# Two row tiles taken in by columns, and a second weight group moved forward

## The chip, the cores and the metric

The kernel runs on one core of one Trainium2 chip. The metric is the device time of one execution in microseconds (us). The core has five engines, each with its own instruction queue that it works through in order: TensorE (PE in the profile), VectorE (DVE), ScalarE (ACT), GpSimd (POOL) and SyncE (SP), which here only issues DMA transfers. Engines wait for each other by semaphores; a transfer runs beside them once it is issued.

## The reference, cut to what matters

```python
# x: 2048 x 512; all in float32
xn = layernorm(x)                                  # per row, no weights
q, k, v = split(xn @ wqkv)                         # wqkv: 512 x 1536, 32 heads of 16
s = attention(q, k, v) @ wo                        # each position sees 8 positions, 2 apart
z = gelu(xn @ w_in)                                # 512 x 1792, two halves z1, z2
g = w_sp @ layernorm(z2) + b_sp                    # w_sp: 2048 x 2048
out = x + s * silu((z1 * g) @ w_out)
```

Only the first two lines matter for this change: the row normalisation of `x` and its product with `wqkv`.

## The kernel before

**Tiles and products.** The 2048 rows are taken as 16 row tiles (`NT`) of 128 rows and 512 columns. A product of float32 precision is made from three matmuls of a rounded "high" part and a "low" remainder: high by high, high by low, low by high. ScalarE makes each high part (a copy with rounding), VectorE each low part (source minus high). A product of one row tile with one weight group (`wqkv` has three groups of 512 columns, `NG`) is 4 blocks of the contraction by 3 = 12 matmuls of 128x512, into one PSUM bank. In the product of a tile, the matmuls that read the tile's high part come first; the first one that reads its low part is the third (in `product`, lines 393 to 397).

**Two ways in.** TensorE wants `xn` with the contraction (the columns of `x`) on the partitions.

- Row tiles 0 to `OPEN - 1` (0 to 5 before) are loaded by rows (`load_x`, line 209). VectorE takes mean and variance (`stats_x`), centres the rows (tiles 0 to 3) or centres and scales them (tiles 4 and 5) in `normal_x`; TensorE transposes them in four pieces (`turned_x`, line 234), ScalarE copies the high part out of PSUM (line 235), VectorE makes the low part (`low_x`, line 240). For tiles 0 to 3 (`JC = 4`) the scale is applied when the product is evicted.
- The later tiles come in twice: by rows for their statistics alone (`fetch_rows`, line 257, and `row_stats`, lines 261 and 262), and by columns from a transposed copy of `x` in DRAM (`fetch_cols`, line 268, tiles `xT`). The statistics of a group of three or four tiles then go round by DRAM: `rows_ready` (lines 272 and 273) turns variances into scales, with the power on GpSimd; `rows_out` transposes them on VectorE (line 244) and stores them with four DMAs (line 246, `mv_d`); `rows_in` (line 277) loads them back, spread over all partitions, as `mr`. With `xT` and `mr` there, `column_tile` does two VectorE operations (line 286) and the high copy on ScalarE (line 289), and `low_x` the low part on VectorE (line 240).

**Order.** Instructions issued under `pin(...)` keep the order in which the code is written, on every engine that they are on. So the place of a statement in this part of the code is its place in the queue of VectorE, ScalarE and SP. The matmuls, evictions and stores inside `pair(g, j0)` (the products of tiles `j0` and `j0 + 1` with weight group `g`) are not pinned; a scheduler places them between the pinned ones when the kernel is built. Buffers: six row tiles for statistics (tag `xs`), four column tiles (tag `xT`), two `mr`. A column tile can be loaded when the tile four before has had its low part taken. Each DMA of SP and ACT also uses one of eight semaphores in turn and waits for the transfer eight before it.

After `opening` (line 301), which takes the first tiles in and starts their products, the code alternates `pair`, statistics and column tiles up to tile 15. Then come the rest of the products with the three groups, the z branch, the spatial product with `w_sp`, and the two output projections; attention runs on VectorE and GpSimd beside them.


## Time and profile before

| | before |
|---|---|
| time, median of 3 runs | 694.22 us (693.69 to 698.0) |
| the profiled execution: its own time, its span | 692.16 us, 690.3 us |
| TensorE busy, of the span | 684.8 us, 99%, 3080 matmuls |
| VectorE / ScalarE / GpSimd busy | 619.8 (90%) / 276.0 (40%) / 216.8 us (31%) |
| DMA | 182.43 MB, mean 264 GB/s |

The span runs from the first instruction to the last of the profiled execution; the rest of its own time, 1.86 us, lies around it. Times in the trace count from the start of the span. A row of the timeline reads: start, duration, engine, line, operation, tile written <- tiles read, and in brackets how long the engine was idle before and what ended it. Matmuls are pipelined, so their durations overlap; the distance between two starts is what one costs. The engine "SPq" or "POOLq" in a row is that engine's issue of a DMA.

### The profile page before, as it was taken

To read this page: it belongs to the slowest core of one execution; us is meant where nothing else is said; L and a number is where in the kernel's file an instruction comes from. 1 tells how busy PE (TensorE), PEld (TensorE's weight loads), DVE (VectorE), ACT (ScalarE), POOL (GpSimd) and SP (SyncE) were. 2 spreads that over 40 slices of the span, in tenths; PEclk is the share of its full clock that TensorE was granted. 3 is DMA by queue.
4 is the path that set the end of the run, shared out by engine and by line. 5 is a ranking of instruction groups with operands and counts; after the bars stand their busy time and mean duration, and the time that the engine had idled before them with its cause. 6 is when DMAs were issued, how large, how long until landed. Compare 5 with 4: busy or idle time off the path is not lost.

```text
span 690.3 us, 9237 instructions
## 1 busy us (share of the span) xinstructions
PE 684.8 (99%) x3080; PEld 572.5 (83%) x3080; DVE 619.8 (90%) x866; ACT 276.0 (40%) x458; POOL 216.8 (31%) x242
## 2 busy tenths in 40 slices
PE   9999999999999999999999999999999999999997
PEld 7888888888888899888888888888888888888886
DVE  6677869999989979798999999999999999999765
ACT  4343334224424256785434544432444444211432
POOL 3105837373443221223323222224021202552320
PEclk9999999999999999999999999999999999999999
DMA  8759899969999865267797859677576692663996
GB/s 281 257 180 299 292 359 388 334 218 370 404 414 355 324 207 180 97 207 249 232 397 285 328 195 319 202 237 262 171 270 238 219 325 89 205 186 126 308 309 252
DMA packets 102223, 182.43 MB, mean 264 GB/s; under 512 B 9184, under 2 KB 45152, under 8 KB 102176
## 3 DMA queue, kind: packets, MB, share of 16 engines
q1 hardware_dynamic: 56624, 102.21, 43.7%
q0 software_dynamic: 13824, 52.24, 20.9%
q10 hardware_dynamic: 31728, 27.40, 11.9%
q8 instruction: 24, 0.39, 0.2%
q14 instruction: 23, 0.19, 0.1%
HBM read 122.49 MB, written 59.32 MB: 263 GB/s over the span
## 4 chain that ended last, share of the span: by engine, by line
PE 99%; DMA 0%; DVE 0%; issue 0%
PE g L848 39%; PE qkv L395 6%; PE qkv L396 6%; PE qkv L397 6%; PE z L751 4%; PE z L750 4%; PE z L715 4%; PE z L714 4%; PE b L1089 4%; PE b L1091 4%; PE b L1090 4%; PE z L716 4%; PE z L749 3%; PE s L1089 2%; PE s L1091 2%; PE s L1090 2%
## 5 line engine op out<-in xcount | busy, mean ns | idle before, releaser
L643 POOL TENSOR_TENSOR pv<-pv 128x1024 f32<-128x1024 f32 x29 | 69.6, 2399 | 94.3 <-DVE pv L630 83.0
L583 DVE TENSOR_TENSOR pr<-k,q 128x2048 f32<-128x2048 f32 x32 | 74.7, 2333 | 1.5 <-DMA k<-qkv_d 1.4
L630 DVE TENSOR_TENSOR pv<-v,lg 128x2048 f32<-128x2048 f32 x32 | 74.5, 2329 | 0.6
L590 DVE TENSOR_REDUCE lg<-pr 128x128 f32<-128x2048 f32 x32 | 72.9, 2279 | 0.1
L657 POOL DMA_DIRECT2D o_d<-tt x32 | 17.9, 560 | 148.0 <-DVE tt L656 104.5
L443 ACT ACTIVATE stage<-qkv 128x512 f32<-128x512 f32 x40 | 23.0, 590 | 31.9 <-DMA qkv_d<-stage 20.2
L1100 ACT ACTIVATE bt<-b 128x512 f32<-128x512 f32 x16 | 9.5, 596 | 45.7 <-PE b L1091 45.7
L830 POOL DMA_DIRECT2D ol<-o_d x32 | 17.7, 554 | 28.9 <-DVE o_1l L204 6.0
L720 ACT ACTIVATE z1t<-z 128x512 f32<-128x512 f32 x28 | 15.5, 596 | 25.8 <-DMA z_d<-z1t 14.1
L761 DVE BATCH_NORM_STATS2 zst<-zt 128x6 f32<-128x448 f32 x32 | 19.3, 610 | 7.0 <-ACT zt L752 7.0
L751 PE MATMUL z<-w_0h,BIG 128*128 128x512 f32 x64 | 25.0, 391 | 0.0
L750 PE MATMUL z<-w_0l,BIG 128*128 128x512 f32 x64 | 25.0, 391 | 0.0
L286 DVE TENSOR_TENSOR xT<-xT,mr 128x512 f32<-128x512 f32 x20 | 14.9, 743 | 11.2 <-DMA mr<-mv_d 6.9
L775 ACT ACTIVATE zt<-zt,nmz,mvz 128x896 f32<-128x896 f32 x16 | 17.4, 1128 | 18.0 <-POOL nmz L769 18.0
L767 POOL TENSOR_TENSOR mvz<-mvz,nhalf 128x2 f32<-128x2 f32 x8 | 9.3, 1157 | 47.3 <-DVE mvz L764 47.3
L749 PE MATMUL z<-w_0h,BIG 128*128 128x512 f32 x60 | 23.3, 389 | 0.0
L648 DVE TENSOR_TENSOR pv<-pv 128x512 f32<-128x512 f32 x32 | 22.9, 714 | 0.0
L752 ACT ACTIVATE zt<-z 128x512 f32<-128x512 f32 (+1 forms) x32 | 16.0, 537 | 15.8 <-DMA sums_d<-sa 12.2
L751 PE MATMUL z<-w_1h,BIG 128*128 128x384 f32 x64 | 21.5, 336 | 0.0
L750 PE MATMUL z<-w_1l,BIG 128*128 128x384 f32 x64 | 21.5, 335 | 0.0
L403 POOL TENSOR_TENSOR sb<-sa,sb 128x512 f32<-128x512 f32 x12 | 19.8, 1647 | 5.4 <-DMA sb<-in_w_sp 5.0
L202 ACT ACTIVATE BIG<-zl 128x512 fp32r<-128x512 f32 x20 | 12.4, 630 | 20.7 <-DVE zl L921 20.6
(480 smaller groups left out, 2262.6 us busy)
## 6 DMA issues: line engine op xcount, KB each, us to landing
qkv_d<-stage ACTq DMA_DIRECT2D x24, 512.0 KB
v<-qkv_d POOLq DMA_DIRECT2D x14, 704.0 KB, 5.0
k<-qkv_d POOLq DMA_DIRECT2D x13, 704.0 KB, 6.3
sums_d<-sa POOLq DMA_DIRECT2D x14, 512.0 KB, 7.6
sums_d<-sb POOLq DMA_DIRECT2D x14, 512.0 KB, 9.4
z_d<-z1t ACTq DMA_DIRECT2D x14, 512.0 KB
zl<-z_d SPq DMA_DIRECT2D x12, 512.0 KB
tr<-t_d SPq DMA_DIRECT2D x12, 384.0 KB
```

The lines of the kernel that those rows point to most:

```text
L395: nc.tensor.matmul(pq, xh[:, k], wh, start=k == 0, stop=False)
L396: nc.tensor.matmul(pq, xh[:, k], wl, start=False, stop=False)
L397: nc.tensor.matmul(pq, xl[:, k], wh, start=False, stop=k == KB - 1)
L583: line(nc.vector.tensor_tensor(pr, taps(ks[u], j0), qb.unsqueeze(1).to_broadcast([P, W, NJ * CS]), op=ALU.mult))
L590: line(nc.vector.tensor_reduce(lgs[u][:, j0 * HS : (j0 + NJ) * HS].rearrange("p i w -> p w i"), pr.rearrange("p w (i d) -> p w i d", d=DH) ...
L630: line(nc.vector.tensor_tensor(pv.rearrange("p w (i d) -> p w i d", d=DH), taps(vs[u], j0).rearrange("p w (i d) -> p w i d", d=DH), lgs[u] ...
L643: eng.tensor_tensor(pv[:, 0:4], pv[:, 0:4], pv[:, 4:8], op=ALU.add)
L749: nc.tensor.matmul(pz, xh[:, k], wh, start=k == 0, stop=False)
L750: nc.tensor.matmul(pz, xh[:, k], wl, start=False, stop=False)
L751: nc.tensor.matmul(pz, xl[:, k], wh, start=False, stop=k == KB - 1)
L848: nc.tensor.matmul(pg, z[a], w[b], start=start and i == 0, stop=stop and i == 2, skip_group_check=seeded)
L1089: nc.tensor.matmul(pp[:, cols], hi, wh, start=k == 0, stop=False)
```

## The change

`OPEN` goes from 6 to 4: row tiles 4 and 5 no longer come in by rows and through TensorE. They are the first group of the second way in: fetched by rows for statistics, fetched by columns, their statistics sent round by DRAM on their own (`rows_out((4, 6))`, `rows_in(4, 6)`), then `column_tile(4)` and `column_tile(5)`. So that TensorE has products meanwhile, `pair(1, 0)` and `pair(1, 2)` (tiles 0 to 3 with the second weight group) are written ahead of `pair(0, 4)`. All later groups (6 to 8, 9 to 12, 13 to 15) keep their members and their order on VectorE, but their loads get new places among the others in SP's queue.

```diff
-OPEN = 6
+OPEN = 4
...
         times(1, (3, 0, 1))
-        x += [load_x(j) for j in range(3, OPEN)]
-        for j in range(OPEN, OPEN + 4):
+        x.append(load_x(3))
+        for j in (4, 5):
             fetch_rows(j)
         raw1 = [fetch(wqkv[:, 1, k, :], GC, f"wqkv_1_{k}") for k in range(3)]
...
-        for j in range(3, OPEN):
-            xt = x[j]
-            stats_x(j, xt)
-            low_x(j - 1, p)
-            normal_x(j, xt)
-            if j - 1 < JC:
-                rstd_x(j - 1)
-            first.append(mm(f"qkv_0_{j - 1}"))
-            left.append(12)
-            times(j - 1, *[(k, 0, i) for i in range(2) for k in range(KB)])
-            p = turned_x(j, xt)
-            times(j - 1, *[(k, 1, 0) for k in range(KB)])
-            row_stats(OPEN + j - 3)
-        low_x(OPEN - 1, p)
-        for j in range(10, 13):
+        for j in (4, 5):
+            fetch_cols(j)
+        for j in (6, 7):
             fetch_rows(j)
-        for j in range(6, 10):
-            fetch_cols(j)
-        rows_ready(6, 9)
-        rows_out((6, 9))
+        stats_x(3, x[3])
+        low_x(2, p)
+        normal_x(3, x[3])
+        rstd_x(2)
...
+        for j in (4, 5):
+            row_stats(j)
+        rows_ready(4, 6)
+        low_x(3, p)
+        times(3, *[(k, 1, 0) for k in range(KB)])
+        rstd_x(3)
+        rows_out((4, 6))
...
     pair(0, 0)
-    rows_in(6, 9)
-    for j in range(13, NT):
-        fetch_rows(j)
+    fetch_rows(8)
+    rows_in(4, 6)
+    fetch_rows(9)
+    for j in (6, 7):
+        fetch_cols(j)
     pair(0, 2)
+    for j in range(6, 9):
+        row_stats(j)
+    rows_ready(6, 9)
+    column_tile(4)
+    rows_out((6, 9))
+    column_tile(5)
+    low_x(4, cols[4])
+    for j in range(10, 13):
+        fetch_rows(j)
+    rows_in(6, 9)
+    fetch_cols(8)
+    pair(1, 0)
     for j in range(9, 13):
         row_stats(j)
     rows_ready(9, 13)
-    pair(0, 4)
+    low_x(5, cols[5])
     column_tile(6)
     rows_out((9, 13))
+    pair(1, 2)
     column_tile(7)
     low_x(6, cols[6])
-    for j in range(10, 12):
-        fetch_cols(j)
+    fetch_cols(9)
     rows_in(9, 13)
-    pair(1, 0)
+    for j in range(13, NT):
+        fetch_rows(j)
+    pair(0, 4)
     for j in range(13, NT):
         row_stats(j)
     rows_ready(13, NT)
     column_tile(8)
     low_x(7, cols[7])
-    fetch_cols(12)
+    for j in (10, 11):
+        fetch_cols(j)
     rows_out((13, NT), (0, JC))
-    pair(1, 2)
+    pair(1, 4)
     column_tile(9)
     low_x(8, cols[8])
     rows_in(13, NT)
+    fetch_cols(12)
     column_tile(10)
     low_x(9, cols[9])
-    pair(1, 4)
```

What that does to the queues, in the rows of the built programs (the numbers in a name are group and tile; a last number is only the buffer's).

TensorE, right after the eight matmuls that read the high part of tile 3, before the change (`xt_4` is the transpose of tile 4, `qkv_0_3` the product of tile 3 with the first weight group):

```order
L316 MATMUL qkv_0_3_267<-wqkv_0_3l_168,BIG_98 128x512
L234 MATMUL xt_4_276<-ident_85,x_4_209 128x128 x4
L316 MATMUL qkv_0_3_267<-wqkv_0_0h_130,BIG_98 128x512
L316 MATMUL qkv_0_3_267<-wqkv_0_1h_144,BIG_98 128x512
L316 MATMUL qkv_0_3_267<-wqkv_0_2h_150,BIG_98 128x512
L316 MATMUL qkv_0_3_267<-wqkv_0_3h_167,BIG_98 128x512
L316 MATMUL qkv_0_4_296<-wqkv_0_0h_130,BIG_98 128x512
```

and the same place with the change (`L397` to `L399` are the lines 395 to 397 of before):

```order
L316 MATMUL qkv_0_3_255<-wqkv_0_3l_168,BIG_98 128x512
L397 MATMUL qkv_1_0_354<-wqkv_1_0h_285,BIG_98 128x512
L397 MATMUL qkv_1_1_368<-wqkv_1_0h_285,BIG_98 128x512
L397 MATMUL qkv_1_2_408<-wqkv_1_0h_285,BIG_98 128x512
L397 MATMUL qkv_1_3_422<-wqkv_1_0h_285,BIG_98 128x512
L316 MATMUL qkv_0_3_255<-wqkv_0_0h_130,BIG_98 128x512
```

The transposes are gone, and tiles 0 to 3 begin with the second weight group where tile 4 stood; tile 4 follows 48 matmuls of that group later.

SP's queue, from the stores of the statistics of tiles 6 to 8 (`mvt_6`) to the load of those of tiles 9 to 12 (`mr_9`), before the change:

```order
L246 DMA mv_d_83<-mvt_6_335 6x32 x4
L277 DMA mr_6_361<-mv_d_83 128x768
L257 DMA x_13_363<-in_x 128x512
L257 DMA x_14_365<-in_x 128x512
L257 DMA x_15_367<-in_x 128x512
L246 DMA mv_d_83<-mvt_9_407 8x32 x4
L268 DMA xT_10_417<-in_x_t 128x512
L268 DMA xT_11_419<-in_x_t 128x512
L277 DMA mr_9_421<-mv_d_83 128x1024
```

and with it:

```order
L246 DMA mv_d_83<-mvt_6_333 6x32 x4
L257 DMA x_10_343<-in_x 128x512
L257 DMA x_11_345<-in_x 128x512
L257 DMA x_12_347<-in_x 128x512
L277 DMA mr_6_349<-mv_d_83 128x768
L268 DMA xT_8_351<-in_x_t 128x512
L246 DMA mv_d_83<-mvt_9_401 8x32 x4
L268 DMA xT_9_441<-in_x_t 128x512
L277 DMA mr_9_443<-mv_d_83 128x1024
L257 DMA x_13_445<-in_x 128x512
L257 DMA x_14_447<-in_x 128x512
L257 DMA x_15_449<-in_x 128x512
```

The rows of tiles 13 to 15 stood ahead of the stores of `mvt_9`, and now stand behind the load of `mr_9`.

VectorE with the change, behind the column operations of tile 6, from the transpose of the statistics of tiles 9 to 12 on; before, the same instructions stand in the same order:

```order
L244 STREAM_TRANSPOSE mvt_9_401<-mvx_94 128x32
L286 TENSOR_TENSOR xT_7_313<-xT_7_313,mr_6_349 128x512 x2
L240 TENSOR_TENSOR BIG_98<-xT_6_311,BIG_98 128x4x128
L261 BN_STATS st_13_481<-x_13_445 128x6
L262 BN_AGGR mvx_94<-st_13_481 128x2
L261 BN_STATS st_14_484<-x_14_447 128x6
L262 BN_AGGR mvx_94<-st_14_484 128x2
L261 BN_STATS st_15_487<-x_15_449 128x6
L262 BN_AGGR mvx_94<-st_15_487 128x2
L272 TENSOR_SCALAR mvx_94<-mvx_94 128x3
L286 TENSOR_TENSOR xT_8_351<-xT_8_351,mr_6_349 128x512 x2
L240 TENSOR_TENSOR BIG_98<-xT_7_313,BIG_98 128x4x128
```

The low part of tile 7 (the last row) stands behind the statistics of tiles 13 to 15, and these now read transfers that are issued behind `mr_9`.

More of the change, by code (lines that the diff above doesn't have):

```diff
@@ L367, in opening @@
         pin(nc.sync.dma_start(raw1[3], wqkv[:, 1, 3, :]))
[L368 to L387 removed]
+        for j in (4, 5):
+            fetch_cols(j)
+        for j in (6, 7):
+            fetch_rows(j)
+        stats_x(3, x[3])
+        low_x(2, p)
+        normal_x(3, x[3])
+        rstd_x(2)
+        left.extend([12, 12])
+        first.append(mm("qkv_0_2"))
+        times(2, *[(k, 0, i) for i in range(2) for k in range(KB)])
+        p = turned_x(3, x[3])
+        times(2, *[(k, 1, 0) for k in range(KB)])
+        first.append(mm("qkv_0_3"))
+        times(3, *[(k, 0, i) for i in range(2) for k in range(KB)])
+        for j in (4, 5):
[5 more added lines that the diff above has]
+        rows_out((4, 6))
         return raw1
@@ L441, in pair @@
         for j in (j0, j0 + 1):
-            pq = first[j] if g == 0 and j < OPEN - 1 else product(g, j, wgs[g])
+            pq = first[j] if g == 0 and j < OPEN else product(g, j, wgs[g])
             nc.scalar.activation(
@@ L457 @@
     pair(0, 0)
+    fetch_rows(8)
[3 more added lines that the diff above has]
+        fetch_cols(j)
+    pair(0, 2)
+    for j in range(6, 9):
[7 more added lines that the diff above has]
+        fetch_rows(j)
     rows_in(6, 9)
-    for j in range(13, NT):
-        fetch_rows(j)
-    pair(0, 2)
+    fetch_cols(8)
+    pair(1, 0)
     for j in range(9, 13):
@@ L517 @@
     for g in range(1, NG):
-        for j in range(OPEN if g == 1 else 0, NT, 2):
+        for j in range(OPEN + 2 if g == 1 else 0, NT, 2):
             if g == 1 and j == NT // 2:
```

## The prediction

> **What bounds the kernel now.** I read the page's busy times and chain first, then TensorE's waits, then the windows of the first 60 us, then each engine's timeline there.
>
> ```profile
> PE 684.8 (99%) x3080; PEld 572.5 (83%) x3080; DVE 619.8 (90%) x866; ACT 276.0 (40%) x458; POOL 216.8 (31%) x242
> PE 99%; DMA 0%; DVE 0%; issue 0%
> PE warm L296 <- POOL ident masks.py:199: 1.3, 1, 1.3
> PE xt L234 <- DVE x L228: 0.3, 1, 0.3
> 16.95:45.00 28.05, 28.05 (x128) 22.85 (x128) 19.17 (x45) 11.27 (x19) 4.19 (x5) 1.00 0.74 241
> 45.00:60.00 15.00, 15.00 (x68) 12.43 (x67) 9.84 (x16) 5.34 (x10) 2.35 (x3) 1.00 0.76 220
> ```
>
> The chain that ended last is TensorE alone. The next two rows are all its waits: 1.6 us, both before the first product. A busy share of 99% could hide gaps, since matmuls overlap, so the pace must be read from starts:
>
> ```profile
> 30.82 0.39 PE L396 MATMUL qkv<-wqkv_1l,BIG 128*128 128x512 f32 x1
> ...
> 40.11 0.39 PE L396 MATMUL qkv<-wqkv_0l,BIG 128*128 128x512 f32 x1
> ```
>
> Between these two rows lie 41 steps: 9.29 / 41 = 0.2266 us per matmul, without a hole. So the kernel is one TensorE stream. A matmul taken out pays its step in full, and a pause put in costs its length in full, wherever it falls. The change can do only these two things. The windows (TensorE, weight loads, VectorE, ScalarE, GpSimd, clock, DMA share, GB/s) say that VectorE is busy 19.17 of 28.05 us where the change acts, and the DMA engines 74%.
>
> **What it removes from TensorE.** Eight transposes, four for each of tiles 4 and 5.
>
> ```profile
> 16.95 0.41 PE L316 MATMUL qkv<-wqkv_0h,BIG 128*128 128x512 f32 x1
> ...
> 18.81 0.60 PE L234 MATMUL xt<-ident,x 128*128 128x128 f32 x4
> 19.17 0.48 PE L316 MATMUL qkv<-wqkv_0h,BIG 128*128 128x512 f32 x1
> 19.48 0.40 PE L316 MATMUL qkv<-wqkv_1h,BIG 128*128 128x512 f32 x1
> L234 PE MATMUL xt<-ident,x x24: 270/273/476, 5.4 to 22.4; 128*128 128x128 f32 x24
> ```
>
> Four transposes take 19.17 - 18.81 = 0.36 us, and the matmul behind them a step of 0.31 instead of 0.23: 0.44 us a tile, 0.89 us for two. The number of 512-wide matmuls stays, so **-0.9 us** is all there is to gain.
>
> The last row gives 273 ns as the length of one transpose. The Trainium skill (TensorE: Matmul & The Clock Gate, Part 4: PE-mode transpose) states some 275 ns for one in a kernel's context, and the row agrees; eight of those would be an estimated 2.2 us. The starts decide here, since the four overlap.
>
> **What it adds elsewhere.** VectorE loses two normalisations (0.54 each) and gains four column operations (about 0.7 each) and one transpose of 0.2: +1.9 us, beside 8.9 idle us in the first window; nothing if no order is disturbed, 1.9 at most. ScalarE keeps its two high copies. GpSimd exchanges two powers for one. SP gains two column loads and a read-back of 256 KB each and four small stores, 0.8 MB against 182; their bytes are nothing, their places in the queue are not.
>
> **What it moves: the low part of tile 7.** In VectorE's queue the statistics of tiles 13 to 15 stand ahead of the column operations of tile 8 and of the low part of tile 7, before and after. Before, their rows were long there. Now SP issues them behind the read-back of tiles 9 to 12, which waits for stores that follow tile 6's column operation, which needs the read-back of tiles 6 to 8, and that follows the one of tiles 4 and 5. Three trips by DRAM in a row, one of them new. TensorE waits for the low part at its 15th matmul from tile 6 on. Both sides of that meeting can be dated.
>
> *When TensorE needs it.* Up to 16.95, the first matmul of tile 3, the streams are alike. From there on stand 12 for tile 3, 48 for tiles 0 to 3 with the second group, 48 for tiles 4 and 5 with both, 12 for tile 6 and 2 for tile 7: 122 x 0.2266 = 27.6 us, so at **44.6 us**.
>
> *When VectorE has it.* The rows:
>
> ```profile
> 16.84 0.69 DVE L240 TENSOR_TENSOR BIG<-xt,BIG 128x512 fp32r<-128x512 f32 x1 [1.17 <-ACT BIG L235]
> 17.45 0.54 DVE L197 TENSOR_SCALAR x<-x,mvx 128x512 f32<-128x512 f32 x1
> 19.70 0.15 DVE L220 TENSOR_SCALAR mvx<-mvx 128x1 f32<-128x1 f32 x1
> 19.93 0.55 POOL L221 TENSOR_TENSOR mvx<-mvx,nhalf 128x1 f32<-128x1 f32 x1 [1.26 <-DVE mvx L220]
> 25.08 0.21 DVE L244 STREAM_TRANSPOSE mvt<-mvx 128x32 f32<-128x32 f32 x1 [0.98 <-POOL mvx L273]
> 25.32 1.34 SPq L246 DMA_DIRECT2D mv_d<-mvt  x4
> 28.57 0.35 SPq L277 DMA_DIRECT2D mr<-mv_d  x1
> 28.97 1.82 SPq L257 DMA_DIRECT2D x<-in_x  x3
> 33.47 1.42 DVE L286 TENSOR_TENSOR xT<-xT,mr 128x512 f32<-128x512 f32 x2 [2.39 <-DMA mr<-mv_d]
> 34.81 0.20 DVE L244 STREAM_TRANSPOSE mvt<-mvx 128x32 f32<-128x32 f32 x1
> ```
>
> 1. The statistics of tiles 4 and 5 leave VectorE (L244) behind the low part of tile 3 (17.45 where L197 stood) and one more power: 19.93 - 19.70 + 0.55 = 0.78, and 0.04 to the transpose: 18.3.
> 2. One trip. From the transpose to the issue of the read-back 28.57 - 25.08 = 3.49; from there to the first column operation 4.90, and 4.09 in the second trip (41.99 to 46.08, below). So 7.6 to 8.4; I take 7.6, since this read-back is the smallest. Tile 4: 25.9.
> 3. Column operation to the next transpose 34.81 - 33.47 = 1.34, and a second trip: tile 6 at 25.9 + 1.3 + 7.6 = 34.8. (The statistics of tiles 9 to 12 stand ahead of it in VectorE's queue; their rows are issued in the same trip, and could add up to 1 us.)
> 4. Again 1.34, and 3.49 to the issue of the third read-back: 39.6.
> 5. The rows of tile 15, the third load behind it:
>
> ```profile
> 41.99 0.33 SPq L277 DMA_DIRECT2D mr<-mv_d  x1
> 46.08 1.42 DVE L286 TENSOR_TENSOR xT<-xT,mr 128x512 f32<-128x512 f32 x2 [4.51 <-DMA mr<-mv_d]
> 51.67 0.75 SPq L277 DMA_DIRECT2D mr<-mv_d  x1
> 57.79 1.42 DVE L286 TENSOR_TENSOR xT<-xT,mr 128x512 f32<-128x512 f32 x2 [3.91 <-DMA xT<-in_x_t]
> 0.72 0.38 SPq L209 DMA_DIRECT2D x<-in_x  x1
> 3.92 0.69 DVE L214 BATCH_NORM_STATS2 st<-x 128x6 f32<-128x512 f32 x1 [2.91 <-DMA x<-in_x]
> ```
>
>    The first load behind a read-back was waited for until 57.79 - 51.67 = 6.1 us after the latter's issue; two more at 1.82 / 3 = 0.61 make 7.3. A load with nothing ahead takes 3.92 - 0.72 = 3.2, and it is issued 0.4 + 1.2 later: 4.8. I take the middle, 6.1: the same traffic, but nothing stands in front of the read-back. 45.7.
> 6. From there:
>
> ```profile
> 38.44 0.66 DVE L261 BATCH_NORM_STATS2 st<-x 128x6 f32<-128x512 f32 x1
> 39.13 0.18 DVE L262 BATCH_NORM_AGGREGATE mvx<-st 128x2 f32<-128x6 f32 x1
> 39.35 0.17 DVE L272 TENSOR_SCALAR mvx<-mvx 128x3 f32<-128x3 f32 x1
> 39.43 1.41 DVE L286 TENSOR_TENSOR xT<-xT,mr 128x512 f32<-128x512 f32 x2
> 40.76 0.68 DVE L240 TENSOR_TENSOR BIG<-xT,BIG 128x512 fp32r<-128x512 f32 x1
> ```
>
>    These are the statistics of tile 15, the columns of tile 8 and the low part of tile 7 of before: 40.76 + 0.68 - 38.44 = 3.0 us. So **48.7 us**.
>
> TensorE would pause 48.7 - 44.6 = **4.1 us** there. Before, tile 6 began at
>
> ```profile
> 42.60 0.39 PE L395 MATMUL qkv<-wqkv_0h,BIG 128*128 128x512 f32 x1
> ```
>
> so the low part of tile 7 was needed at 42.60 + 14 x 0.2266 = 45.8 and was there at 41.4. That cover of 4.4 us is what the change spends.
>
> **Other places.** Tile 4's high part, at 25.9 + 1.4 + 0.6 = 27.9, meets a need at 16.95 + 60 x 0.2266 = 30.5; its low part (29.4) one at 31.4. Tile 5's low part, behind the statistics of tiles 9 to 12, comes at 35 to 36 against 36.8: close, but a wait there would shorten the later one by as much. The second group's weights are loaded earlier and split from 16.8 on, and TensorE's first use is at 18.8. After the pause VectorE needs 1.34 + 0.60 = 1.9 us a tile and TensorE 12 x 0.2266 = 2.7, so it gains ground; the column loads of tiles 11 to 13 are issued behind the same low part and come about when they are needed: 0 to 1 us more, of which I count nothing. The rest of the program has the same work in nearly the same order.
>
> **The sum.** -0.9 + 4.1 = +3.2. The profiled execution took 692.16 us (span 690.3, and 1.86 around it): 695.4 on its scale. The median of the runs, 694.22, is 2.06 higher than that execution, so on its scale **697.4 us**, +0.5%. Bounds of the pause: with both trips at 8.4 and 7.3 in step 5, 51.6 and so 7.0 us; with stores that land at once and loads of 3.2 (a trip of 0.24 + 1.34 + 3.2 = 4.8) the low part is there at about 40, and there is no pause.
>
> **Rivals.**
>
> *No pause.* The early traffic is thinner than before (rows of tiles 8 to 15 no longer stand in front of everything), so the trips may be short enough. Each of the three must then save 1.4 us on the shortest row. For it: the read-backs are small. Against it: the undelayed trip of the trace took 8.4, 7.6 is already pieced from its parts and the next one's, and the windows show the DMA engines 74% busy. It gives -0.9: 693.3.
>
> *A long pause, and a slow TensorE behind it.* After its idle start TensorE runs slower for a while:
>
> ```profile
> 5.40 1.12 PE L234 MATMUL xt<-ident,x 128*128 128x128 f32 x4 [0.28 <-DVE x L228]
> 6.31 1.06 PE L296 MATMUL warm<-ident 128*128 128x128 f32 x4
> ```
>
> Four transposes took 6.31 - 5.40 = 0.91 us there against 0.36 later; TensorE had begun at 1.35. For it: 8.4 is a trip as measured, and two such make the upper bound. If that pause brings the same 5.0 us back at 0.36 / 0.91 of the pace, 3.0 us are lost on top: -0.9 + 7.0 + 3.0 = +9.1, or 703.3. It decides from a pause long enough to count as idle; the trace shows no pause in the stream that could tell how long that is, and the granted clock reads 1.00 in all windows, so no row tells when the pace falls. The Trainium skill (TensorE: Matmul & The Clock Gate, Part 1: The HAM clock gate) puts it at one idle window of about 3.4 us that runs free of the kernel, and the slow pace at half for about as long; an estimate by that is 1.7 us lost, seldom at a pause of 4.1. The slow start agrees with it; no run here shows the rest.
>
> *It doesn't matter, because the order after it moves too.* The scheduler puts some later instructions elsewhere, at the end too, where TensorE's last late step hung on a copy of ScalarE:
>
> ```profile
> 677.80 0.61 ACT L202 ACTIVATE o_3h<-ol 128x512 fp32r<-128x512 f32 x1
> 678.47 0.50 PE L1089 MATMUL s<-BIG,o_3h 128*128 128x512 f32 x1
> 678.81 0.39 PE L1090 MATMUL s<-BIG,o_3h 128*128 128x512 f32 x1
> ```
>
> A step of 0.34 instead of 0.23: the order was just in time there. I give such places 0.3 us either way in all: 697.1 to 697.7.
>
> **Chances.** The pause of 2 to 6 us, as forecast: 0.62, 1 to 5 us slower. No pause, or one under 2 us: 0.24. The long one: 0.14, of which rather more than half passes 1%. A measurement of this kernel can tell about 1% (6.9 us) from no change, so faster by more than that 0.01 (the gain is bounded at 0.9), within 0.90, slower 0.09. The range: downward to the case without a pause, 693.3, and half the 2 us between the two scales, so 692.5; upward to the pause at its upper bound, 700.3, and a little of the lost pace: 701.
>
> **What would show it.** In the changed kernel's profile: 16 transposes of line 234; among TensorE's waits one of about 4 us near 44.6 for the low part of a column tile (line 240), at the second product behind tile 5's; on VectorE an idle stretch of 4 us or more before statistics (line 261), ended by the rows of `x`; the read-back's issue near 39.6. If TensorE's waits stay as they are, steps 2 to 5 are too long; if the pause is at tiles 4 or 5, the first trip is. A longer step between matmuls behind the pause would be the second rival.

## The result, and the profile after

The change made the kernel slower: 711.18 us (median of 6 runs, 709.93 to 713.73) against 693.96 us for the kernel before, a ratio of 1.0239 (95% interval 1.020 to 1.0277). The profiled execution took 711.61 us, its span grew from 690.3 to 709.6. Forecast were 697.4 us and a range of 692.5 to 701.

The page's busy times and the chain that ended last; then all of TensorE's waits (total us, how many, the longest):

```profile
PE 688.5 (97%) x3072; PEld 574.0 (81%) x3072; DVE 619.0 (87%) x868; ACT 278.3 (39%) x458; POOL 216.8 (31%) x241
PE 58%; DVE 17%; DMA 16%; issue 4%; ACT 3%; POOL 1%; SPq 1%; ACTq 0%; DVEq 0%
```

```profile
PE qkv L399 <- DVE BIG L240: 7.9, 2, 7.4
PE g L867 <- ACT g L885: 6.3, 2, 4.9
PE warm L296 <- POOL ident masks.py:199: 1.3, 1, 1.3
PE z L768 <- ACT z1t L739: 0.8, 1, 0.8
PE xt L234 <- DVE x L228: 0.7, 1, 0.7
PE qkv L316 <- ACT BIG L235: 0.2, 1, 0.2
```

TensorE, alone on the chain before, holds 58% of it now. The first wait is the forecast one, for the low part of a column tile (line 240). The second and the fourth stand hundreds of microseconds behind the change; for all such places the forecast had 0.3 us either way.

The pause in TensorE's timeline, and what follows it:

```profile
45.18 0.39 PE L398 MATMUL qkv<-wqkv_0l,BIG 128*128 128x512 f32 x1
52.97 0.79 PE L399 MATMUL qkv<-wqkv_0h,BIG 128*128 128x512 f32 x1 [7.40 <-DVE BIG L240]
53.56 0.63 PE L397 MATMUL qkv<-wqkv_1h,BIG 128*128 128x512 f32 x1
53.99 0.63 PE L398 MATMUL qkv<-wqkv_1l,BIG 128*128 128x512 f32 x1
...
55.70 0.46 PE L399 MATMUL qkv<-wqkv_2h,BIG 128*128 128x512 f32 x1
56.00 0.39 PE L397 MATMUL qkv<-wqkv_3h,BIG 128*128 128x512 f32 x1
```

The next matmul was due at 45.41 and came at 52.97: 7.6 us lost. Then the steps are 0.43 us instead of 0.23 until 55.70, another 1.4 us. Far behind, at the start of the spatial product, are TensorE's rows of the second wait, and ScalarE's:

```profile
307.48 0.40 PE L867 MATMUL g<-wsp_0h,BIG 128*128 128x512 f32 x1
312.73 0.80 PE L867 MATMUL g<-wsp_0h,BIG 128*128 128x512 f32 x1 [4.85 <-ACT g L885]
...
318.45 0.49 PE L867 MATMUL g<-wsp_1l,BIG 128*128 128x512 f32 x1
307.83 0.58 ACT L771 ACTIVATE zt<-z 128x512 f32<-128x512 f32 x1
311.06 1.13 ACT L794 ACTIVATE zt<-zt,nmz,mvz 128x896 f32<-128x896 f32 x1 [2.65 <-POOL nmz L788]
312.10 0.58 ACT L885 ACTIVATE g<-b_a 128x512 f32<-128x512 f32 x1
```

Before TensorE may add to a bank of `g`, ScalarE copies a start value into it (`g<-b_a`, line 885; four banks). The fourth copy stands here behind the normalisation of a z tile (line 794), and that waits 2.65 us for GpSimd. In ScalarE's timeline of before the same copy stood ahead of that normalisation:

```profile
294.04 0.59 ACT L752 ACTIVATE zt<-z 128x512 f32<-128x512 f32 x1
294.66 0.60 ACT L866 ACTIVATE g<-b_a 128x512 f32<-128x512 f32 x1
...
297.25 2.16 ACT L775 ACTIVATE zt<-zt,nmz,mvz 128x896 f32<-128x896 f32 x2 [0.83 <-POOL nmz L769]
```

Every step of TensorE's that was too long, added up from its starts over the whole trace:

| place | us lost |
|---|---|
| 36.7: tile 5's low part | 0.6 |
| 45.2: tile 7's low part (the forecast pause) | 7.6 |
| 53 to 56: slow steps behind it | 1.4 |
| 225: start of z2 | 0.9 |
| 305 and 307: third and fourth bank of `g` | 1.6 + 5.0 |
| 313 to 318: slow steps behind it | 2.9 |
| eight transposes less (forecast) | -0.9 |
| sum; measured growth of the span | 19.1; 19.3 |

So 9.6 us are lost in the front and 10.4 behind it.

### The profile page after: what moved, and what is told of

It reads as the page before. It is cut to its first block, busy times and chain, and to the rows that moved or that the text cites. A ratio compares the mean times of both kernels' runs of the same rounds, so it can differ in the third digit from the quotient of the medians.

```text
span 709.6 us, 9239 instructions
## 1 busy us (share of the span) xinstructions
PE 688.5 (97%) x3072; PEld 574.0 (81%) x3072; DVE 619.0 (87%) x868; ACT 278.3 (39%) x458; POOL 216.8 (31%) x241
## 4 chain that ended last, share of the span: by engine, by line
PE 58%; DVE 17%; DMA 16%; issue 4%; ACT 3%; POOL 1%; SPq 1%; ACTq 0%; DVEq 0%
PE g L867 38%; DMA qkv_d<-stage 6%; DMA sb<-in_w_sp 4%; PE b L1110 4%; PE b L1109 4%; PE b L1108 4%; DVE pr L602 2%; PE s L1110 2%; PE s L1109 2%; PE s L1108 2%; DVE lg L609 2%; PE qkv L316 1%; DMA x<-in_x 1%; DMA sums_d<-sa 1%; DMA w_0r<-in_w_in 1%
## 5 line engine op out<-in xcount | busy, mean ns | idle before, releaser
L602 DVE TENSOR_TENSOR pr<-k,q 128x2048 f32<-128x2048 f32 x32 | 76.4, 2387 | 2.1 <-DMA k<-qkv_d 1.9
L739 ACT ACTIVATE z1t<-z 128x512 f32<-128x512 f32 x28 | 15.5, 596 | 38.4 <-DMA z_d<-z1t 18.4
L204 DVE TENSOR_TENSOR BIG<-zt,BIG 128x512 fp32r<-128x512 f32 (+2 forms) x24 | 18.6, 773 | 8.1 <-ACT BIG L202 8.1
L399 PE MATMUL qkv<-wqkv_0h,BIG 128*128 128x512 f32 x44 | 17.7, 401 | 7.9 <-DVE BIG L240 7.9
L405 POOL TENSOR_TENSOR sb<-sa,sb 128x512 f32<-128x512 f32 x12 | 18.5, 1540 | 12.7 <-DMA sb<-in_w_sp 12.5
L286 DVE TENSOR_TENSOR xT<-xT,mr 128x512 f32<-128x512 f32 x24 | 16.4, 684 | 6.2 <-DMA xT<-in_x_t 3.8
L202 ACT ACTIVATE BIG<-zl 128x512 fp32r<-128x512 f32 x20 | 12.4, 631 | 23.5 <-DVE zl L940 23.4
```

The lines of the kernel that those rows point to most:

```text
L602: line(nc.vector.tensor_tensor(pr, taps(ks[u], j0), qb.unsqueeze(1).to_broadcast([P, W, NJ * CS]), op=ALU.mult))
```

## The experiments

Spans are those of each kernel's profiled execution (before: 690.3). Single executions of one slower kernel differ by several us (spans of 707.9 to 711.7 for the changed kernel, 705.8 to 715.0 for `low_first`), so small differences between such spans mean little; the waits inside one trace are what is compared. The ratio to the kernel before comes from runs on the same chip.

### Is the pause the wait for late rows?

`rows_early` issues the rows of tiles 13 to 15 earlier:

```diff
-    for j in range(10, 13):
+    for j in range(10, NT):
         fetch_rows(j)
     rows_in(6, 9)
...
     rows_in(9, 13)
-    for j in range(13, NT):
-        fetch_rows(j)
```

> The changed kernel (span 709.6) with one edit: the rows of tiles 13 to 15 are issued on SP with those of tiles 10 to 12, ahead of the read-back of tiles 6 to 8, not behind that of tiles 9 to 12. Theory 'late rows' (the pause of 7.6 us at tile 7's low part is the wait of VectorE's statistics for these rows): VectorE then has the low part of tile 7 about 5.5 us behind tile 6's column operation, which three more loads put off from 37.7 to 39 or 40, so at 45 to 46 against a need of 45.2: a pause under 1.5 us, and no stretch of matmuls at 0.43 us behind it; the front gives back 7.5 to 9 us. Rival 'third trip' (what TensorE waits for is the chain of three trips, whose rows are only its last link): the pause stays over 4 us. For the middle of the program: in this kernel ScalarE's queue has the fourth start value of the g products (g<-b_a) ahead of tile 6's normalisation (zt). Theory 'order' (the 6.6 us lost there come from the place of that copy in ScalarE's queue) and theory 'lag' (they come from VectorE running late since the front) both say that they go; span 692 to 696 by either.

Measured: the pause at tile 7 was 1.7 us, without slow steps. But the span was 703.6, the ratio 1.0248 (1.0218 to 1.0278): TensorE now waited 4.8 us in z1 (163 us) and 3.3 us at z2 (235 us), with 3.8 us of slow steps behind them, and not at `g`. 'Late rows' held for the front. What both theories said of the middle was wrong: the waits had moved.

`low_first` leaves the loads and moves VectorE's work:

```diff
     pair(0, 4)
+    column_tile(8)
+    low_x(7, cols[7])
     for j in range(13, NT):
         row_stats(j)
     rows_ready(13, NT)
-    column_tile(8)
-    low_x(7, cols[7])
```

> The changed kernel with one edit: on VectorE the column operation of tile 8 and the low part of tile 7 stand ahead of the statistics of tiles 13 to 15, not behind; all loads stay where they are. 'Late rows': the low part of tile 7 is there at about 43.5, so the pause at 45.2 goes; VectorE then waits for the rows until 49.9 with tile 9 behind them, and tile 8's low part or tile 9 may be late instead: TensorE needs tile 8's 2.7 us after tile 7's, at 48 to 49, tile 9's at 51; a wait of 1 to 3 us there. The front gives back 5 to 8 us. 'Third trip': the pause moves to tile 8 or 9 nearly whole and gives back under 3. In the middle this kernel's queue of ScalarE has the fourth start value behind both normalisations of tiles 6 and 14. 'Order' says a pause of 6 to 8 us there, more than the 5.3 of the changed kernel; 'lag' says none or under 2, since VectorE is no longer late. Span by 'late rows' with 'order' 702 to 706, by 'late rows' with 'lag' 693 to 697.

Measured: no pause at tile 7, one of 5.5 us one tile later, at tile 8's low part (46.9), with 2.8 us of slow steps; span 708.3, ratio 1.0286 (1.0229 to 1.0342). The pause moved nearly whole, as the rival 'third trip' said, and against the 1 to 3 us of 'late rows'. The last link is still the same: VectorE stood until 46.56 at the statistics of tiles 13 to 15, waiting for their rows, and tile 8's low part stood behind them. The rows are late because the third trip is. No wait at `g` either, though the fourth copy stood further back than in the changed kernel; instead 4.0 us in z1 and 3.6 at z2, with 3.1 us of slow steps.

### Order or lag?

`seed_first` and `before_seed_late` move the fourth start value alone, one kernel each way:

```diff
-                for ins in (highs[-1], combined[HT - 3]):
+                for ins in (highs[-1], combined[HT - 3], normals[HT - 2]):
                     tc.add_manual_dep(ins.ins, last_seed.ins.name, NOSYNC, ...)
```

> The changed kernel with one edit in the middle of the program: the fourth start value of the g products (g<-b_a on ScalarE) must stand ahead of the normalisation of tile 6. Nothing changes up to 290 us, nor in the order of TensorE. 'Order': the pause of 5.3 us at the fourth bank falls to 1.3 or less (the copy can run at 308.4 to 309.0, when the z eviction ahead of it is done, against a need of 307.7), and the 11 steps at 0.43 us behind it (2.6 us) go as well; the first pause there (1.6) stays; span 702 to 704. 'Lag': the copy waits for what is ahead of it anyway, and the span stays at 708 to 710.

Measured: the wait at the fourth bank fell from 5.0 to 1.4 us, the third's stayed (1.4), slow steps were 1.7 instead of 2.9; span 706.7, ratio 1.0226 (1.0193 to 1.0259). The queue's order made most of that wait, but the slow steps behind two pauses so close did not go.

> The kernel before (span 690.3) with one edit: the fourth start value stands behind the normalisation of tile 6 on ScalarE, where the changed kernel has it, and TensorE's order there is held as it was. The front is untouched. 'Order': TensorE waits at 296.3 until that copy, which then runs at 298.3 to 298.9: a pause of 2.6 us, no slow matmuls behind it, span 693. The rest of the changed kernel's 5.3 would be lag of VectorE and GpSimd. 'Lag' alone: no pause over 0.5 us, span 690 to 691.

Measured: a pause of 2.2 us at 296.0, as by 'order', and slow steps of 1.7 us a little later, which I had excluded; another 1.2 us at 681, where the order had moved too; span 695.5, ratio 1.0053 (1.0035 to 1.0071).

The place of one instruction was thus worth a wait of 2 to 4 us. To try the whole order, the next kernels carry a table: for each engine, the sequence in which the other kernel's built program has the instructions behind the front (all those after the last column tile; both kernels issue the same ones). Each is tied to its predecessor:

```diff
+                ins = tc.nc.get_inst_by_name(name)
+                if behind:
+                    tc.add_manual_dep(ins, behind, NOSYNC, reason="the order of the other kernel")
+                behind = name
```

> The changed kernel with its own first 60 us (up to the scaling of the column-summed tiles), and behind them the order of instructions of the kernel before, engine by engine, held by a table of numbers; the work is the same. Theory 'order' (the waits at the starts of z1, z2 and g come from where the scheduler puts instructions once the front has changed): only the losses of the front are left, -0.9 + 0.6 + 7.6 + 1.4 us, so a span of 699, and no wait of TensorE over 0.6 us behind 60 us. 'Lag' (they come from VectorE, ScalarE and GpSimd arriving late from the front): over 4 us of waits stay behind 60 us, span 703 or more.

> The crossing the other way: the kernel before with its own first 60 us, and behind them the order that the changed kernel has. 'Order': TensorE waits where the changed kernel does, 1 us at the start of z2 and 4 to 7 us at the third and fourth bank of g, with a stretch of slow matmuls behind it: span 695 to 700. 'Lag': no waits, span 690 to 691.

TensorE's waits in `after_old_order` (the table shifts the lines: L521 and L362 are the L399 and L240 of above), then in `before_new_order`:

```profile
PE qkv L521 <- DVE BIG L362: 7.4, 1, 7.4
PE warm L418 <- POOL ident masks.py:199: 1.3, 1, 1.3
```

```profile
PE g L971 <- ACT g L989: 4.3, 1, 4.3
PE z L872 <- ACT z1t L843: 2.1, 1, 2.1
PE qkv L518 <- DVE BIG L361: 1.4, 2, 1.1
PE z L837 <- ACT z1t L843: 1.4, 1, 1.4
```

The changed front with the old order: one pause, 7.6 us, 2.2 us of slow steps, and nothing behind 60 us; span 698.6, ratio 1.0124 (1.0111 to 1.0137). The front of before with the new order: 705.0, ratio 1.0188 (1.0174 to 1.0201), with waits at z1, z2 and `g` and 3.4 us of slow steps, though its front has only 1.7 us of waits, near 60 us, that before has not. The order alone, without the change, loses more than the changed front does. (The table by itself costs little: `second_group_first`, below, carries it too, at a ratio of 1.001.)

Later, with a front that hardly pauses (`loads_spread`, below, 691.3), the table was taken away:

> loads_spread (span 691.3) without the table that holds the order of the kernel before behind the front: the scheduler orders the rest itself. 'Order': the front stays as it was (one pause of about 2 us at tile 8), and waits of 1 to 7 us come back at the starts of z1, z2 or g, as in every version here that the scheduler ordered with a changed front: span 696 to 705. 'Lag' alone: no front so close to that of before can bring them, span 691 to 692.

```profile
PE g L866 <- ACT g L884: 6.9, 2, 4.9
PE qkv L399 <- DVE BIG L240: 1.9, 1, 1.9
PE warm L296 <- POOL ident masks.py:199: 1.4, 1, 1.4
PE z L767 <- ACT z1t L738: 1.3, 1, 1.3
```

Span 703.7, ratio 1.0193 (1.0168 to 1.0217): the same front, 12.4 us slower by the order in which the scheduler leaves the rest. So the order behind the front is a cause, shown both ways. It is not the only one: some fronts below leave waits in z1 and z2 although they hold the old order.

### What makes the trips long?

A trip goes from the transposed statistics by four small stores of SP to DRAM and back as a broadcast read (`mr`). SP's and VectorE's rows of the second trip in the changed kernel:

```profile
26.84 1.29 SPq L246 DMA_DIRECT2D mv_d<-mvt  x4
28.97 1.30 SPq L257 DMA_DIRECT2D x<-in_x  x3
30.43 0.34 SPq L277 DMA_DIRECT2D mr<-mv_d  x1
31.81 0.69 DVE L261 BATCH_NORM_STATS2 st<-x 128x6 f32<-128x512 f32 x1 [2.27 <-DMA x<-in_x]
34.11 0.69 DVE L261 BATCH_NORM_STATS2 st<-x 128x6 f32<-128x512 f32 x1 [1.39 <-DMA x<-in_x]
35.77 0.69 DVE L261 BATCH_NORM_STATS2 st<-x 128x6 f32<-128x512 f32 x1 [0.75 <-DMA x<-in_x]
36.79 0.69 DVE L240 TENSOR_TENSOR BIG<-xT,BIG 128x512 fp32r<-128x512 f32 x1
37.73 1.42 DVE L286 TENSOR_TENSOR xT<-xT,mr 128x512 f32<-128x512 f32 x2 [0.25 <-DMA mr<-mv_d]
```

From the first store to the column operation: 10.9 us, 7.3 of them from the issue of the read-back on. But VectorE waited only 0.25 us for the read-back itself. Ahead of tile 6's column operation its queue has the statistics of tiles 9 to 12 and tile 5's low part. It waited 4.4 us there for the rows of tiles 10 to 12, which SP issued at 28.97 in the same trip, and was through at 37.48. Two things thus ended together, and a quicker read-back alone would have brought tile 6 forward by 0.25 us. In `after_old_order` and `stores_later` VectorE comes to that column operation later than the read-back: it waits for the rows alone, and its time says of the read-back only that it took no longer.

The windows (last two columns: DMA engines' share, GB/s), first of after, then one of before:

```profile
18.00:21.00 3.00, 3.00 (x15) 2.48 (x14) 2.78 (x6) 1.59 (x4) 0.19 (x1) 1.00 0.07 16
29.00:37.70 8.70, 8.24 (x37) 6.54 (x36) 3.89 (x10) 2.33 (x4) 0.74 (x1) 1.00 0.88 276
37.70:41.60 3.90, 3.90 (x18) 3.17 (x19) 3.37 (x6) 2.12 (x4) 0.65 (x1) 1.00 0.08 24
41.60:50.00 8.40, 3.97 (x18) 2.96 (x16) 1.83 (x5) 1.31 (x3) 0.00 (x0) 0.94 0.93 285
```

```profile
18.00:21.00 3.00, 3.00 (x17) 2.35 (x16) 2.67 (x8) 1.15 (x2) 1.09 (x2) 1.00 1.08 381
```

The DMA engines stand still while SP waits for statistics, and are full once a trip is let go, because the loads that stood behind it leave with it. Before, 381 GB/s were moved at 18 to 21 us, when the changed kernel moved 16. Five kernels test what that does to the second trip, all with the old order behind the front.

`rows_10_12_early` issues those three loads before the trip's stores; `stores_later` takes two stores of 0.5 MB out of ScalarE's queue and issues them from GpSimd after the trip; `extra_bytes` puts 0.77 MB in front of the read-back:

```diff
     for j in (6, 7):
         fetch_cols(j)
+    for j in range(10, 13):        # rows_10_12_early: here, and not ahead of rows_in(6, 9)
+        fetch_rows(j)
...
     rows_ready(9, 13)
+    for dst, sv in held:           # stores_later: pair(0, 2) and pair(1, 0)
+        for b in (0, NBLK // 2):
+            pin(nc.gpsimd.dma_start(dst[:, b : b + NBLK // 2], sv[:, b : b + NBLK // 2]))
...
+    for j in range(10, 13):        # extra_bytes
+        again = ep.tile([P, D], F32, tag="again", name=f"again_{j}", bufs=3)
+        pin(nc.sync.dma_start(again, xr[j]))
     rows_in(6, 9)
```

> The changed kernel with the order of before behind the front (after_old_order, span 698.6), and one edit: the rows of tiles 10 to 12 are issued behind the columns of tile 7, not right ahead of the second read-back. 'Bursts': 0.77 MB at the 280 GB/s of that stretch are 2.7 us, so the second read-back takes 4.6 to 5.5 us instead of 7.3, tile 6 is there near 35, the rows of 13 to 15 are issued 2 to 2.5 us earlier, and the pause at tile 7 falls from 7.6 to 5 or 5.5: span 695.5 to 696.5. 'Three trips': the read-back still takes about 7, the span stays over 698.

> As after_old_order, and the two stores of 0.5 MB (stage of tiles 2 and 3 with the first group, tiles 0 and 1 with the second) that ScalarE issues beside the second read-back are issued by GpSimd (in halves) behind the power for tiles 9 to 12, after that read-back. 'Bursts': the second read-back takes 5 to 5.5 us instead of 7.3; the stores then run beside the third, whose rows become later by up to 2 us, so the pause at tile 7 is 6 to 8 and the span 697 to 699. If the read-back still takes 7 us, the stores do not matter to it and the rows of tiles 10 to 12 do alone.

> As after_old_order (span 698.6), with 0.77 MB put in front of the second read-back: the rows of tiles 10 to 12 are loaded a second time, into buffers of their own that nothing reads. 'Bytes' (a trip's time is what the DMA engines need for everything issued ahead of it): at 280 GB/s 2.7 us more, so the second read-back reaches VectorE near 40.5 instead of 37.7, and the pause at tile 7 grows from 7.6 to about 10. 'Issue' (only SP's time in issuing counts): three issues of 0.43 are 1.3 us, tile 6 at 39, the pause under 9.

The second trip's rows in `rows_10_12_early`, then in `extra_bytes` (L368, L399, L408 are the L246, L277, L286 of above):

```profile
27.40 4.97 SPq L368 DMA_DIRECT2D mv_d<-mvt  x4
34.14 0.34 SPq L399 DMA_DIRECT2D mr<-mv_d  x1
37.69 1.42 DVE L408 TENSOR_TENSOR xT<-xT,mr 128x512 f32<-128x512 f32 x2 [4.40 <-DMA mr<-mv_d]
```

```profile
27.04 1.71 SPq L368 DMA_DIRECT2D mv_d<-mvt  x4
30.66 2.45 SPq L599 DMA_DIRECT2D again<-in_x  x3
33.16 0.49 SPq L399 DMA_DIRECT2D mr<-mv_d  x1
39.28 1.42 DVE L408 TENSOR_TENSOR xT<-xT,mr 128x512 f32<-128x512 f32 x2 [2.52 <-DMA mr<-mv_d]
```

In `rows_10_12_early` the read-back fell from 7.3 to 3.6 us, as 'bursts' said; but the four small stores now took SP 4.97 us instead of 1.29: behind the first of them SP waited 3.4 us, by the profile until a store of `stage` that ScalarE had issued landed. VectorE was through with what stands ahead at 33.3 and waited 4.4 us for the read-back. The trip as a whole stayed at 10.3. A kernel with these rows early and ScalarE's stores out of the way as well was not run. The pause was 8.7 us, the span 707.2, the ratio 1.0247 (1.0222 to 1.0272), with waits of 3.0 us each in z1 and at z2: my figure for the pause (5 to 5.5) failed.

In `extra_bytes`, with 0.77 MB more in front, the trip took 12.2 us instead of the 10.0 of `after_old_order`, the waits of the front 9.6 instead of 7.6: 2.0 to 2.2 us, between 'bytes' (2.7) and 'issue' (1.3). The rows show it ahead of the read-back: SP took 2.45 us to issue the three loads, not 1.3, and the read-back, once issued, took 6.1 us, no longer than the 6.5 at most of `after_old_order`. Why the issues took so long is not shown; span 701.8, ratio 1.0154 (1.014 to 1.0168).

In `stores_later` the trip took 9.9 us and the pause was 6.7 us; since VectorE waited there for rows, the run doesn't decide what the stores do to the read-back; span 701.2, ratio 1.0171 (1.0137 to 1.0204).

In `trips_by_gpsimd` GpSimd issues stores and read-backs, so that SP's loads no longer stand behind the trips; `spread_by_gpsimd` is the same on `loads_spread`, `before_by_gpsimd` on the kernel before:

```diff
-            pin(nc.sync.dma_start(
+            pin(nc.gpsimd.dma_start(
                 mv_d[j0:j1, :, a * Q : (a + 1) * Q].rearrange("j a q -> (j a) q"),
...
-        pin(nc.sync.dma_start(
+        pin(nc.gpsimd.dma_start(
             mr, mv_d[j0:j1].unsqueeze(0).to_broadcast([P, j1 - j0, 2, P])
```

> As after_old_order (span 698.6, pause 7.6 us), with one edit: the four small stores and the read-back of each trip are issued by GpSimd, in its own DMA queue, not by SP. Theory 'held queue' (SP issues in order, and each trip stands in its queue: its small stores wait for earlier loads to land, and the loads behind wait for the trip): the loads of rows and columns go out as soon as their buffers are free, rows 13 to 15 before 36 us, the second trip takes 4 issues of 0.55 + 2 for the landing + 4 = 8 us and brings tile 6 at 34 to 35; no pause at tile 7; span 689.4 to 692. Rival 'full DMA engines' (a trip is long since its packets stand behind the loads' packets in the DMA engines, whichever queue they come from): the second trip still takes 10 us or more, tile 6 comes at 37 or later, and TensorE pauses 3 us or more somewhere between 40 and 60.

> loads_spread (span 691.3, a pause of 1.8 us at tile 8) with the trips issued by GpSimd as well. 'Held queue': tile 6 near 34, no pause, span 689.4 to 690 and a ratio of 0.998 to 1.000. 'Full DMA engines': the pause of 1 to 3 us stays, span 691 to 692.

> The kernel before with its trips issued by GpSimd, and its own order behind the front. Both theories: TensorE did not wait, so nothing is gained: span 690 to 691, unless GpSimd's issues of 0.55 us each make a trip longer than the 4.4 us of cover, which would show as a wait between 40 and 62.

Measured: the second trip took 10.1 us here too (first store 30.15, read-back 35.08, column operation 40.20), now with the DMA engines only 0.44 and 0.57 busy from 25 to 34 us, but 0.91 and 0.88 from 34 to 41.6, while the read-back ran. GpSimd's four stores took 2.1 us to issue and 2.8 more until the read-back could go. The rows of tiles 13 to 15 were early, and the pause at tile 7 fell to 1.7 us; beside it TensorE waited 1.2 us at tile 6's two parts, 2.4 us at tile 8's low part, behind the third trip, and 3.6 us in z1: span 703.9, ratio 1.018 (1.0161 to 1.0199).

'Held queue' failed with its 8 us and its span; the rival was right on the trip and on tile 6 (40.2), and wrong in that no single pause reached 3 us. `spread_by_gpsimd` gave 698.6 and 1.0124 (1.0109 to 1.0138), with pauses of 1.5 us at 30.2 and 4.5 us at 49.5, against both theories; the control on the kernel before gave 694.7 and 1.0079 (1.0051 to 1.0107), with no wait in its front but 2.0 and 0.8 us in z1. So SP's queue alone does not make the trip long: in a queue of its own it took as long. What part of it is the chain of small transfers and what part the bytes beside it stays open.

### Can the change pay?

`rows_early_old_order` and `both_old_order` (the latter with `low_first`'s edit too) hold the old order behind an earlier front. `loads_spread` rearranges it further: rows 10 to 12 behind the columns of tile 7, six buffers for columns, the columns of 8 and 9 and the rows of 13 to 15 right behind the second read-back, the columns of 12 ahead of the last trip.

> The changed kernel with the rows of tiles 13 to 15 issued ahead (rows_early), and behind the front the order of the kernel before. 'Order': the front loses the 1.9 us seen in rows_early and gains the 0.9 of the transposes; the waits of 4.8 and 3.2 us at z1 and z2 of rows_early go with their slow stretches: span 691 to 692. 'Lag': they stay, since they stood behind a front that hardly paused: span 700 to 704.

> As rows_early_old_order, and tile 8's column operation and tile 7's low part ahead of the statistics of tiles 13 to 15 on VectorE. 'Late rows' and 'order' together: no pause in the front (tile 7's low part 2.1 us earlier than in rows_early, where it missed by 1.7), so what is left is the eight transposes: span 689.4 to 690, 0.1% under the kernel before. If anything else in the front is late it shows as a wait of TensorE between 40 and 60 us.

> The front rearranged, the order of the kernel before behind it: on SP the rows of tiles 10 to 12 are issued behind the columns of tile 7, before the stores of the second trip; the columns of tiles 8 and 9 (six buffers for columns, not four) and the rows of 13 to 15 right behind the second read-back; the columns of tile 12 ahead of the last trip's stores; on VectorE tile 8's columns and tile 7's low part ahead of the statistics of 13 to 15. Theory 'bursts' (the changed kernel's trips take long because each read-back is issued together with the loads that SP held back while it waited, so that the DMA engines are idle, 0.07 and 0.08 of the time, and then full, 0.88 and 0.93): the second read-back takes 4.5 to 5.5 us from issue to the column operation, not 7.3, tile 6 comes near 34 and tile 9 near 42, TensorE waits nowhere in the front, and the span is 689.4 to 690.5, the eight transposes under the kernel before. Theory 'three trips' (the trips are long by themselves): the second read-back still takes over 6.5 us, and TensorE waits 3 us or more between 40 and 60.

`rows_early_old_order`: span 698.9, ratio 1.0133 (1.012 to 1.0146). The pause at tile 7 was 1.7, as seen; but 2.2 us at tile 11's low part, 1.9 + 1.3 us at z1 and z2 and 1.2 us at 405 came in its place. So 'lag' has a share. It isn't only that TensorE is less held up here: `rows_10_12_early` waited in z1 and z2 behind a pause of 8.7 us. Why some fronts leave such waits and `after_old_order` leaves none is not shown.

`both_old_order`: 696.7, ratio 1.0092 (1.0074 to 1.011), with 0.8, 2.3 and 2.7 us at the low parts of tiles 6, 8 and 11, against my 689.4 to 690.

`loads_spread`: 691.3, ratio 1.0021 (1.0012 to 1.003), with one pause, 1.8 us, at tile 8's low part, and nothing behind. That is the sum: 690.3 - 0.9 + 1.8 = 691.2. Its second trip still took 11.4 us: the read-back took 5.0 of them, as 'bursts' said, but SP had waited 3.7 us behind the first small store, so tile 6 came at 38.4 and not near 34. Only more was ready before it.

`tuned_front` puts tile 8's low part behind the statistics of tile 13, each later low part directly behind its column operation, and the columns of 13 ahead of the last trip:

> loads_spread with its last pause (1.8 us at tile 8's low part, which stood behind the statistics of tiles 13 to 15 and a power on VectorE) taken away: tile 8's low part goes behind the statistics of tile 13, from tile 9 on each low part directly behind its column operation, and the columns of tile 13 are issued ahead of the last trip's stores. If the front was all that was left, TensorE waits nowhere and the span is 689.4 to 690.0, ratio 0.998 to 1.0: the 0.9 us of the eight transposes. If tiles 9 to 13 (needed every 2.7 us, made every 2.6) miss, waits of 0.3 to 1 us show between 50 and 62 and the span is 690 to 691.5.

Measured: 0.6 us of wait in the front, and yet a span of 699.0, ratio 1.0113 (1.0095 to 1.0131): 3.7 us in z1 with 1.5 of slow steps, and 0.7 to 1.2 us at three other places. The low parts of tiles 11 and 12 came 3.5 and 4.2 us later than in `loads_spread`, and GpSimd's first sums 3.5 (58.8 against 55.3). Whether that made the wait in z1 is not shown; other versions with such a distance had none. No version beat the kernel before.

One half of the change by itself, in the kernel before and with its order: tiles 0 to 3 meet the second group before tile 5's first product.

```diff
     rows_ready(9, 13)
-    pair(0, 4)
     column_tile(6)
...
     pair(1, 2)
+    pair(0, 4)
     column_tile(9)
```

> Half of the change: the kernel before (six tiles turned by TensorE), but tiles 0 to 3 meet the second group ahead of tile 5's first product and tiles 4 and 5 after it, with the order of before behind the front. By every theory the loads and trips stay where they are, so TensorE waits nowhere: span 690.0 to 690.8. If TensorE does wait, this half has a share in the loss.

Measured: ratio 1.001 (1.000 to 1.002), a span of 692.2 with 0.5 us of wait at 66.8 and 0.3 at 679.8. With the old order held, this half costs next to nothing; the front's loss comes from tiles 4 and 5 by columns. Which half makes the scheduler order the rest anew was not run.

## Why the prediction was wrong

- **-0.9 us for the transposes: borne out as far as a sum can show it.** `loads_spread` and `after_old_order` come within 0.1 and 0.6 us of their spans with it.
- **The pause: right in place and cause, too short.** It had 0.62 for 2 to 6 us; at 7.6 it lies above that and above its upper bound of 7.0. It stands at the 15th matmul from tile 6 on, in front of statistics that wait for `x`, as said. It was needed at 45.4 (forecast 44.6; 0.6 of that is tile 5's low part) and was there at 52.9 (forecast 48.7):

```profile
25.27 1.42 DVE L286 TENSOR_TENSOR xT<-xT,mr 128x512 f32<-128x512 f32 x2 [1.73 <-DMA mr<-mv_d]
...
39.06 0.20 DVE L244 STREAM_TRANSPOSE mvt<-mvx 128x32 f32<-128x32 f32 x1
41.62 0.34 SPq L277 DMA_DIRECT2D mr<-mv_d  x1
49.88 0.69 DVE L261 BATCH_NORM_STATS2 st<-x 128x6 f32<-128x512 f32 x1
52.23 0.68 DVE L240 TENSOR_TENSOR BIG<-xT,BIG 128x512 fp32r<-128x512 f32 x1
```

  Step 2 (tile 4 at 25.9) came at 25.3, step 4 took 2.6 us from the transpose instead of 3.5, step 6 took 3.0 as forecast. **Step 3 failed**: from tile 4's column operation to tile 6's it took 12.5 us instead of 8.9. Two of its terms were too small by nearly the same amount. The read-back, pieced as 4.09 us, took 7.3; and the statistics of tiles 9 to 12, which "could add up to 1 us", held VectorE, with tile 5's low part behind them, until 37.48, 2.7 us behind the 34.8 of the forecast. Either alone would have made tile 6 late. **Step 5 failed** too: 8.3 us from the read-back's issue to tile 15's rows instead of 6.1. -0.6 + 3.5 - 0.9 + 2.2 is the 4.2 us between 48.7 and 52.9; that steps 2 and 4 erred the other way and hid 1.5 us is luck. The reason for 7.6, "since this read-back is the smallest", holds for the first trip only, and "the same traffic" was wrong: three loads stood right ahead of the second read-back, and the loads that before had run at 18 to 21 us ran now beside each trip. My upper bound, 8.4 a trip, was a lighter trip's as well.
- **Slow TensorE behind a long pause: given 0.14, and it happened**, 1.4 us in the front. The granted clock of the window 53 to 56 us:

```profile
53.00:56.00 3.00, 3.00 (x8) 2.37 (x9) 2.93 (x6) 0.63 (x1) 0.00 (x0) 0.53 0.38 89
```

  The size, 3.0 us by the start's pace, was too high; the 1.7 us worked out from the Trainium skill (TensorE: Matmul & The Clock Gate, Part 1: The HAM clock gate) is near the 1.4 here and the 2.2 of `after_old_order`.
- **"The rest of the program has the same work in nearly the same order": the step that cost most.** I gave it 0.3 us either way; it cost 10.4 in the trace. The work is the same, the order is not, and `after_old_order` puts that at 11.0 us of span (709.6 to 698.6), 1.2% of time. The forecast weighed whether instructions moved, not which cover each had. The fourth start value had run 1.0 us ahead of its need (done at 295.3, needed at 296.3).
- Even with that step right, the front alone would have passed the range: 1.0124 of 694.22 is 702.8. (The lower end of the range, by its own terms, comes to 692.3 and not 692.5; nothing hangs on it.)

## What to carry to other kernels

Where a scheduler orders the program, a local change can re-order all that lies behind it, and a place in a stream without gaps can have as little cover as the 1.0 us here: price that as a risk of its own, and tell it from the change itself by holding the order and crossing it both ways. A trip by DRAM is priced with all that will be issued around it, not by the row of a lighter one; look for windows in which the DMA engines stand still because an in-order queue waits. Before a long transfer is blamed for a late instruction, look in the brackets how long its engine waited for it: 7.3 us of read-back were 0.25 us of wait here. In `low_first` a pause of TensorE's was moved, not removed, by reordering its last link.

## What the runs showed of the hardware

Over all traces here, TensorE lost a further 1.4 to 2.9 us in slow steps behind every one of 17 pauses of 3.3 us or more, behind two of nine pauses from 2.2 to 3.0 us (1.7 each), and behind no shorter one that stood alone; two of 1.4 us, 2 us apart, did it once. The Trainium skill (TensorE: Matmul & The Clock Gate, Part 1: The HAM clock gate) has the pace fall after a whole idle window of about 3.4 us that runs free of the kernel. By that a pause of 3.3 to 5 us should often go unpunished; none did here, and the two of 2.2 us are shorter than such a window. The measurement decides against the rule as stated. Whether the window is shorter here, or one that is idle only in part counts too, these runs don't tell.

A small store can cost its queue more than its bytes: the four stores of a trip took SP 1.3 us in the changed kernel and 5.0 us in `rows_10_12_early` and `loads_spread`, where 3.4 and 3.7 us of that were one wait for another transfer to land.
